# Attention products with v on eight 64x32 tiles, and row maxima packed into five banks

## The chip, the cores and the metric

The kernel runs on one core of a Trainium2 chip. The metric is the device time of one execution, in microseconds. Engines are named as in the profile: PE (TensorE, the matrix products), PEld (its weight loads), DVE (VectorE), ACT (ScalarE), POOL (GpSimd) and SP (SyncE, which here issues most transfers). PSUM, where products land, has eight banks of 512 fp32 columns on 128 partitions.

## The reference

Two layers, each an attention block and a feed-forward block, on 2048 rows of width 640. The attention has 32 heads of width 20 and a causal window of 256 keys.

```python
def _A_ref(x, wqkv, wo):                      # attention
    qkv = (x @ wqkv).reshape(B, S, 3, H, Dh)  # H = 32, Dh = 20
    scores = einsum("bhqd,bhkd->bhqk", q, k) * (Dh ** -0.5)
    mask = (i_q - i_k >= 0) & (i_q - i_k < 256)
    p = softmax(where(mask, scores, -1e9))
    o = einsum("bhqk,bhkd->bhqd", p, v)
    return o.reshape(B, S, D) @ wo

def _B_ref(x, w1, b1, w2, b2):                # feed-forward, F = 1536
    r = relu(x @ w1 + b1)
    return (r * r) @ w2 + b2

x = A_x
for _ in range(2):
    x = x + _A_ref(layernorm(x), A_wqkv, A_wo)
    x = x + _B_ref(layernorm(x), B_w1, B_b1, B_w2, B_b2)
```

## The kernel before

The rows are cut into units of 256; units 0 to 7 are the first layer and 8 to 15 the second. In a unit u with u % 8 != 0 a query sees keys of the unit before and of its own; units 0 and 8 start the sequence and see their own keys only. Heads go in groups of four, called a quad here and in the code; there are eight quads in a unit. A quad's four heads are two values of j (columns of a step) by two values of e (the lower or upper 64 partitions, where its q and k lie, 60 rows deep: each value is kept as fp16 parts).

Each quad goes through three steps:

- `max_quad` (the maxima): scores with queries on the partitions. For each of the four w (j and half i of the unit's queries) and each e, 128 queries by 384 keys land in PSUM, a mask is added and DVE takes the row maximum (L592, `tensor_tensor_reduce` over 384 columns). They use two tiles `bb` of three banks each (`bb6`, handed out by `banks()`, which waits for every earlier reader). From unit 2 on they run on four 64x64 tiles of the array (L570), each with the 320 keys that its 64 queries can see; in unit 1 on the whole array (L579).
- `exp_quad` (the scores for the exponentials): scores again, transposed, keys on the partitions, with the negated maxima as two more rows (L647 on four tiles, L655 on the whole array). ACT takes the exponential out of PSUM (L669), POOL zeroes the masked corners (L684, L688). It uses the same six banks.
- `pv_quad` (the products with v): for each block of 128 keys kb and each of the four heads a product of 32 columns of v (20, one for the sum, the rest unused) with the exponentials, in fp32, on four 128x32 tiles (L718). All of it accumulates in one bank `pv`, which ACT copies to `ot` (L730); every second quad SP writes `ot` out. `steps_of` gives the blocks of keys: first block 1 of the unit before (256 queries), then block 0 of the unit before and block 3 (the second block of the own unit), 128 queries each, then block 2 (the first of the own unit), 256.

Between these steps the dense products of other units run: q, k and v of the unit after, the output product and the feed-forward block of the unit before (`mm3`, L261). The order on every engine is written out by a planner in the program itself: `post` puts a job with an estimated cost on a list, `pump` issues jobs in the order of estimated times and priorities, `need` moves the estimated time on until a job is done. The engines then run their orders as fast as the data allows. In `together` a quad's turn is: `exp_quad(n)`, a share `SHARE` of the dense products, `max_quad` for a quad some way ahead, `pv_quad(n)`, the rest of the dense products. Six banks belong to `bb`, two to everything else (`mm_tile`).

`by_tiles` sorts a quad's products so that the one whose tile has the fewest columns queued so far comes first:

```python
for k, (tile, cols, put) in enumerate(pieces):
    order.append((at.get(tile, 0), k, put))
    at[tile] = at.get(tile, 0) + cols
for _, _, put in sorted(order, key=lambda o: o[:2]):
    for e in range(2):
        put(e)
```

Of the kernel before, what the change touches and what calls it, by code (L numbers as in the profile page):

```python
# [16 lines left out]
P = 128  # L17
S = 2048
D = 640
F = 1536  # L20
H = 32
DH = 20
# [22 lines left out]
def kernel(ctx: ExitStack, tc: tile.TileContext, x, wqkv, wo, w1, b1, w2, b2, out):  # L45
# [18 lines left out]
                            fill=NEG, base=2 * P, channel_multiplier=1)  # L64
    b1s = sb.tile([P, FC], F32, name="b1s")
# [288 lines left out]
    def ln_t(u, yT=None):  # L354
        ys = lns.pop(u)
        if yT is None:
            yT = sb.tile([P, 2, KC, T], F16, name="yT", tag="yT", bufs=1)
        yTs[u], pre[u] = yT, []
        bb = banks() if u == 0 else (None, None)
        for i in range(2):  # L360
            yield from split_t(ys[i][0], yT[:, :, :, i * P:(i + 1) * P], ys[i][1], pre[u], bb[i])
# [156 lines left out]
    bb6 = [ps.tile([P, 3, 512], F32, name=f"bb{e}") for e in range(2)]  # L518

    def banks():  # L520
        need(*bbjobs)
        bbjobs.clear()
        return bb6
# [5 lines left out]
    def by_tiles(pieces):  # L529
# [5 lines left out]
        for _, _, put in sorted(order, key=lambda o: o[:2]):  # L535
            for e in range(2):
                put(e)

    def max_quad(n):

        u, qd = divmod(n, NQ)
        g = u % NG
        qt, cur, prev = qts[u], kts[u % 3], kts[(u - 1) % 3]
# [5 lines left out]
        bb = banks()  # L549

        pieces = []
        for w in (3, 0, 1, 2):
            j, i = divmod(w, 2)
            p = 2 * qd + j
            parts = [(prev, 0, T, 0), (cur, 0, P, T)] if i == 0 else [(prev, P, T, 0), (cur, 0, T, P)]
            if g == 0:
                parts = parts[1:]
            if w == 3:
                parts = [(kt, z, z + P, c + z - a) for kt, a, b, c in parts for z in range(a, b, P)]
            if quarters(u):  # L560
                for kt, a, b, c in parts:
                    for h in range(2):
                        a_, b_ = max(a, a + P // 2 * h - c), min(b, a + 5 * P // 2 + P // 2 * h - c)
                        c_ = c + a_ - a

                        def put(e, kt=kt, a=a_, b=b_, c=c_, h=h, w=w, p=p, i=i):
                            r, rows = slice(64 * e, 64 * e + 3 * DH), slice(64 * h, 64 * (h + 1))
                            to = (bb[e][rows, c // P, 3 * P + c % P:3 * P + c % P + b - a] if w == 3
                                  else bb[e][rows, w, c:c + b - a])
                            nc.tensor.matmul(to, qt[r, p, i * P + 64 * h:i * P + 64 * (h + 1)], kt[r, p, a:b],  # L570
                                             start=True, stop=True, tile_position=(64 * e, 64 * h))

                        pieces.append((h, b_ - a_, put))
                continue
            for kt, a, b, c in parts:
                for e in range(2):
                    r = slice(64 * e, 64 * e + 3 * DH)
                    to = bb[e][:, c // P, 3 * P:] if w == 3 else bb[e][:, w, c:c + b - a]
                    nc.tensor.matmul(to, qt[r, p, i * P:(i + 1) * P], kt[r, p, a:b], start=True, stop=True)  # L579
        by_tiles(pieces)  # L580
        now[0] += (763.0 if quarters(u) else 870.0) if g else 440.0
        for w in range(4):
            j, i = divmod(w, 2)
            o = (0 if g else T if i == 0 else P)
            for e in range(2):
                accum = mx[:, e, (2 * qd + j) % (2 * GQ), i:i + 1]
                if w == 3:
                    v, mask = bb[e][:, o // P:, 3 * P:], maskb[:, o:].rearrange("p (a n) -> p a n", n=P)
                else:
                    v, mask = bb[e][:, w, o:3 * P], maskb[:, o:]  # L590
                bbjobs.append(post("D", 113 + 1.047 * (3 * P - o), lambda v=v, mask=mask, accum=accum:
                                   nc.vector.tensor_tensor_reduce(out=v, in0=v, in1=mask, scale=1.0, scalar=-3.0e38,  # L592
                                                                  op0=ALU.add, op1=ALU.max, accum_out=accum),
                                   prio=urgency["turn"]))
# [32 lines left out]

    def exp_quad(n):
# [3 lines left out]
        bb = banks()  # L632
# [4 lines left out]
        for k, st in enumerate(steps):  # L637
            o = 0
            for kb, kt, ko, q0, qn in st:
                w = qn * P  # L640
                for j in range(2):
                    for h in range(2 if quarters(u) else 0):
                        a, b = (0, w - 64 * (1 - h)) if kb < 2 else (64 * h, w)

                        def put(e, k=k, kt=kt, ko=ko, q0=q0, j=j, h=h, o=o, a=a, b=b):
                            r, rows = slice(64 * e, 64 * e + 3 * DH + 2), slice(64 * h, 64 * (h + 1))
                            nc.tensor.matmul(bb[e][rows, k, o + a:o + b],  # L647
# [4 lines left out]
                        pieces.append((h, b - a, put))  # L652
                    for e in range(0 if quarters(u) else 2):
                        r = slice(64 * e, 64 * e + 3 * DH + 2)
                        nc.tensor.matmul(bb[e][:, k, o:o + w], kt[r, 2 * qd + j, ko:ko + P],  # L655
# [5 lines left out]
        for k, st in enumerate(steps):  # L661
            pts, ms = [], []
            for e in range(2):
# [3 lines left out]
                def power(k=k, e=e, o=o, box=box):  # L667
                    box["pt"] = sb.tile([P, 512], F32, name="pt", tag="pt", bufs=6)
                    nc.scalar.activation(box["pt"][:, :o], bb[e][:, k, :o], AF.Exp, scale=SCALE / (QS * QS))  # L669

                ex = post("A", 50 + 0.834 * o, power, prio=urgency["turn"])
                bbjobs.append(ex)
# [31 lines left out]
    def pv_quad(n, quad):  # L704
        u, qd = divmod(n, NQ)
        steps = steps_of(u)
        pv, jobs = mm_tile([P, T], "pv")
        for k, pts in enumerate(quad[0]):
# [27 lines left out]

        jobs.append(post("A", 262, out, prio=0))
        if qd % 2:
# [395 lines left out]
```

## Time and profile before

| what | value |
|---|---|
| median of 3 runs | 1613.28 us (1612.49 to 1613.58) |
| profiled execution | 1611.7 us, of it a span of 1609.9 us from the first to the last instruction |
| PE busy, share of the span | 1573.4 us, 98% |
| DVE, ACT, POOL busy | 65%, 46%, 38% |
| granted TensorE clock | 1.0 |
| DMA | 158.56 MB, 98 GB/s on average |

A row of the profile gives the line of the program, the engine, the operation, what it writes and reads by the program's names, the shape and the number of records; then the busy time, the mean length of one in ns and the idle time of the engine ahead of it with what ended it. A product's row also gives the tile of the array (rows * columns). An fp32 product is recorded as two. Records of products overlap, so that a mean length is longer than the distance from one to the next. "Issue" in a chain is time in which an engine waited for nothing that the profile shows.

### The profile page before, as it was taken

The numbers are of one execution on the slowest core, as the hardware profiler recorded it, in microseconds if no ns is written. First come the engines' busy times: TensorE is split into PE (matmuls) and PEld (weight loads), VectorE is DVE, ScalarE is ACT, GpSimd is POOL, SyncE is SP. The second block draws the span as 40 slices with busy tenths as digits, with TensorE's granted clock in tenths as the row PEclk, the third lists the DMA queues.
The fourth block names the chain that finished last, engine by engine and source line by source line (L and its number), as shares of the span: only waits on it lengthen the run. The fifth ranks groups of instructions, "written<-read, shape, count | busy, mean of one in ns | idle before, by whom it ended". The sixth has DMA issues, their size and how long they took to land.

```text
span 1609.9 us, 51896 instructions
## 1 busy us (share of the span) xinstructions
PE 1573.4 (98%) x21222; PEld 1178.3 (73%) x21222; DVE 1044.4 (65%) x3250; ACT 734.3 (46%) x1593; POOL 610.9 (38%) x1288
## 2 busy tenths in 40 slices
PE   8998999999999999999999999999999999998999
PEld 7676767777777777777777777777777777775667
DVE  8786865666757657665556766567675666757441
ACT  4554535344453444545343453534545444453522
POOL 1224434235353443535223352533534334353512
PEclk9999999999999999999999999999999999999999
DMA  9763243352434424343352534334343352431020
GB/s 270 206 169 103 60 121 80 99 127 50 120 84 111 97 67 119 74 121 80 95 133 54 122 80 124 81 95 111 66 115 86 107 109 52 111 73 55 27 65 18
DMA packets 234246, 158.56 MB, mean 98 GB/s; under 512 B 82200, under 2 KB 217752, under 8 KB 234008
## 3 DMA queue, kind: packets, MB, share of 16 engines
q1 hardware_dynamic: 227640, 145.74, 37.2%
q10 hardware_dynamic: 6368, 9.50, 2.0%
q8 instruction: 167, 2.74, 0.8%
q14 instruction: 71, 0.58, 0.1%
HBM read 84.68 MB, written 52.95 MB: 85 GB/s over the span
## 4 chain that ended last, share of the span: by engine, by line
PE 90%; DVE 4%; ACT 3%; issue 1%; DMA 1%; POOL 1%; SPq 0%; DVEq 0%; POOLq 0%; ACTq 0%
PE acc L261 67%; PE pv L718 10%; PE bb L647 4%; PE bb L570 4%; DVE bb L592 2%; ACT pt L669 1%; PE spin L275 1%; PE tr L605 1%; PE bb L655 1%; PE bb L579 1%; DMA od<-o 0%; ACT r L889 0%; DVE mx L592 0%; POOL pt L688 0%; DVE mT L610 0%
## 5 line engine op out<-in xcount | busy, mean ns | idle before, releaser
L592 DVE CUSTOM_DVE_ANT_0 bb<-bb,maskb 128x384 f32<-128x384 f32 (+2 forms) x1024 | 510.6, 566 | 101.0 <-PE bb L570 76.1
L669 ACT ACTIVATE pt<-bb 128x512 f32<-128x512 f32 (+1 forms) x736 | 375.8, 601 | 231.2 <-PE bb L647 199.5
L684 POOL TENSOR_SCALAR_AFFINE_SELECT pt<-pt 128x256 f32<-128x256 f32 x448 | 196.9, 445 | 556.2 <-ACT pt L669 534.3
L261 PE MATMUL acc<-y,w_s 128*128 128x256 f16 x2880 | 330.4, 273 | 4.5 <-DVE y L311 1.5
L261 PE MATMUL acc<-w_s,hh 128*128 128x320 f16 x2304 | 326.2, 299 | 0.0
L261 PEld LDWEIGHTS <-w_s 128*128 128x128 f16 x2880 | 277.4, 98 | 57.2 <-issue 23.5
L261 PEld LDWEIGHTS <-hh 128*128 128x128 f16 x2304 | 221.6, 98 | 96.9 <-issue 12.5
L261 PEld LDWEIGHTS <-wq_s 128*128 128x128 f16 x2400 | 230.6, 98 | 45.7 <-issue 15.2
L261 PE MATMUL acc<-yT,wq_s 128*128 128x256 f16 x2250 | 258.9, 273 | 3.6 <-ACT ot L730 1.6
L688 POOL TENSOR_SCALAR_AFFINE_SELECT pt<-pt 128x256 f32<-128x256 f32 x512 | 218.9, 450 | 94.0 <-ACT pt L669 93.1
L899 DVE TENSOR_TENSOR hh<-r,hh 128x256 f16<-128x256 f32 x192 | 92.6, 505 | 201.3 <-ACT hh L896 195.0
L718 PE MATMUL pv<-pt,vt 128*32 128x128 f32 (+1 forms) x3840 | 186.7, 329 | 2.7 <-DVE x L828 1.7
L893 POOL TENSOR_TENSOR r<-r 128x256 f32<-128x256 f32 x192 | 113.5, 612 | 179.0 <-ACT r L889 177.6
L730 ACT COPY ot<-pv 128x256 f32<-128x256 f32 x128 | 47.6, 372 | 276.6 <-PE pv L718 276.5
L592 DVE DVE_READ_ACCUMULATOR2_ANT mx<- 128x1 f32 x1024 | 144.4, 141 | 0.0
L261 PE MATMUL acc<-wo_s,od 128*128 128x320 f16 x960 | 138.7, 300 | 2.1 <-ACT od L801 1.3
L261 PE MATMUL acc<-wq_s,yT 128*128 128x320 f16 x900 | 132.2, 299 | 3.6 <-DVE y L311 1.9
L718 PEld LDWEIGHTS pv<-pt,vt 128*32 128x32 f32 x3840 | 103.5, 109 | 44.0 <-POOL pt L688 5.7
L889 ACT ACTIVATE r<-acc,b1s 128x256 f32<-128x256 f32 x192 | 80.5, 471 | 98.6 <-PE acc L261 95.8
L261 PEld LDWEIGHTS <-od 128*128 128x128 f16 x960 | 91.4, 98 | 44.7 <-issue 6.0
L261 PEld LDWEIGHTS <-yT 128*128 128x128 f16 x900 | 86.6, 98 | 41.1 <-issue 10.5
L298 POOL TENSOR_TENSOR bmv<-bmv,neghalf 128x1 f32<-128x1 f32 x64 | 43.8, 691 | 138.7 <-DVE bmv L292 137.9
(86 smaller groups left out, 1229.0 us busy)
## 6 DMA issues: line engine op xcount, KB each, us to landing
qt<-qk SPq DMA_DIRECT2D x30, 480.0 KB
kt<-qk SPq DMA_DIRECT2D x30, 480.0 KB
qk<-qd SPq DMA_DIRECT2D x17, 640.0 KB
o<-ot SPq DMA_DIRECT2D x256, 42.0 KB
od<-o SPq DMA_DIRECT2D x14, 640.0 KB
qk<-yl SPq DMA_DIRECT2D x13, 640.0 KB
qk<-qd SPq DMA_DIRECT2D x17, 320.0 KB
xt<-in_A_x_dram SPq DMA_DIRECT2D x16, 320.0 KB
```

Source lines behind the costliest of these rows:

```text
L261: nc.tensor.matmul(acc, lhs(a, c), rhs(b, c), start=(k == 0), stop=(k == 3 * nk - 1))
L570: nc.tensor.matmul(to, qt[r, p, i * P + 64 * h:i * P + 64 * (h + 1)], kt[r, p, a:b], start=True, stop=True, tile_position=(64 * e, 64 * h))
L592: nc.vector.tensor_tensor_reduce(out=v, in0=v, in1=mask, scale=1.0, scalar=-3.0e38, op0=ALU.add, op1=ALU.max, accum_out=accum),
L647: nc.tensor.matmul(bb[e][rows, k, o + a:o + b], kt[r, 2 * qd + j, ko + 64 * h:ko + 64 * (h + 1)], qt[r, 2 * qd + j, q0 * P + a:q0 * P + b] ...
L669: nc.scalar.activation(box["pt"][:, :o], bb[e][:, k, :o], AF.Exp, scale=SCALE / (QS * QS))
L684: nc.gpsimd.affine_select(out=m, in_=m, pattern=[[0, 2], [-1, P]], compare_op=ALU.is_gt, fill=0.0, base=0, channel_multiplier=1)
L688: nc.gpsimd.affine_select(out=m, in_=m, pattern=[[0, 2], [1, P]], compare_op=ALU.is_ge, fill=0.0, base=0, channel_multiplier=-1)
L718: nc.tensor.matmul(pv[32 * jj:32 * (jj + 1), q0 * P:(q0 + qn) * P], vf[:, c:c + 32], pj[:, j, :], start=(k == 0), stop=(k == len(steps) - ...
L730: nc.scalar.copy(ot[:, qd % 2], pv)
L889: nc.scalar.activation(box["r"], acc[:, f, :], AF.Relu, bias=b1s[:, f0 + f:f0 + f + 1], scale=1.0 / (YS * WS))
L893: nc.gpsimd.tensor_tensor(box["r"], box["r"], box["r"], op=ALU.mult)
L899: nc.vector.tensor_sub(hh[:, 1, f, :], box["r"], hh[:, 0, f, :])
```

## The change

**Products with v.** In units with u % 8 != 0 the keys of a block are split into two halves h of 64 partitions, and each half has its own bank: the lower half `pv`, the upper half `sixth`. There are eight tiles of 64 rows by 32 columns, one for each half and head. Each half streams only the queries that can see it (`seen`, the windows that the exponentials' scores have already). After ACT's copy of `pv` to `ot`, a new DVE job adds `sixth` to it; the output write waits for that addition.

**Banks.** The two tiles of three banks become one of five (`five`) and one of one (`sixth`). The scores for the exponentials use them as before (`sbank`), but the last bank has a list of readers of its own (`sixjobs`, awaited by `last_bank`).

**Maxima.** In units with u % 8 != 0, unit 1 now included, the eight results of a quad are packed: 320 columns each instead of 384, in five banks, where the second half of the queries sees keys shifted by 64, so that one packed mask (`maskq`, made once) serves all. A result can cross a bank. One bank holds results of both e; the products that write it for one e run first (`TURN`), and 256 columns of w = 0 are left for later: `rest`, called at the head of the next `pv_quad`, runs them on 64x32 tiles ahead of the products with v and posts the eight maxima. So their DVE jobs are posted in `pv_quad`, after all products of the maxima.

**Share.** `SHARE` goes from 0.55 to 0.52, so that less dense work lies between the scores and the maxima, and more behind the products with v.

The diff, cut to its core:

```diff
+    maskq = sb.tile([P, 5 * Q], BF16, name="maskq")
...
-    bb6 = [ps.tile([P, 3, 512], F32, name=f"bb{e}") for e in range(2)]
+    five = ps.tile([P, 5, 512], F32, name="five")
+    sixth = ps.tile([P, 512], F32, name="sixth")
+    flat = five.rearrange("p a n -> p (a n)")
+    sbank = [[five[:, 0], five[:, 1], five[:, 2]], [five[:, 3], five[:, 4], sixth]]
...
+    TURN = ((3, 2, 1, 0), (1, 2, 3, 0))
+    LATER = 4 * Q
+    def max_pieces(n, e, w, x0, x1, m):
...
+        p, at, r = 2 * qd + j, 5 * Q * (4 * e + w), slice(64 * e, 64 * e + 3 * DH)
+        cuts = sorted({x0, x1, *(z - at for z in range(0, 5 * 512, 512) if x0 < z - at < x1)})
...
+                            nc.tensor.matmul(flat[t * m:(t + 1) * m, o:o + b - a],
+                                             qt[r, p, i * P + t * m:i * P + (t + 1) * m],
+                                             kt[r, p, a + to:b + to], start=True, stop=True,
+                                             tile_position=(64 * e, t * m))
...
     def max_quad(n):
...
+        if u % NG:
...
+            by_tiles([x for e in range(2) for w in TURN[e]
+                      for x in max_pieces(n, e, w, LATER if w == 0 else 0, 5 * Q, Q)])
+            now[0] += 656.0
+            def rest():
+                by_tiles([x for e in range(2) for x in max_pieces(n, e, 0, 0, LATER, P // 4)])
+                now[0] += 110.0
+                for e, w in ((0, 3), (1, 3), (0, 2), (1, 2), (0, 1), (1, 1), (0, 0), (1, 0)):
+                    reduce(flat[:, 5 * Q * (4 * e + w):5 * Q * (4 * e + w + 1)], maskq, accum[e, w], 5 * Q)
+                mxjobs[u, G] = list(bbjobs)
+            rest_of.append(rest)
+            return
...
+    def seen(kb, h, w):
+        return (0, w - Q * (1 - h)) if kb < 2 else (h * Q, w)
...
     def exp_quad(n):
-        bb = banks()
+        banks()
+        last_bank()
...
-                bbjobs.append(ex)
+                (sixjobs if (k, e) == (2, 1) else bbjobs).append(ex)
...
     def pv_quad(n, quad):
+        while rest_of:
+            rest_of.pop()()
         pv, jobs = mm_tile([P, T], "pv")
+        if u % NG:
+            last_bank()
+            two = (pv, sixth[:, :T])
+            for k, pts in enumerate(quad[0]):
+                need(*quad[1][k])
...
+                                    nc.tensor.matmul(two[h][32 * jj:32 * (jj + 1), q0 * P + a:q0 * P + b],
+                                                     vf[h * Q:(h + 1) * Q, c:c + 32], pj[:, j, a:b], start=(kb == 1),
+                                                     stop=(k == len(steps) - 1), skip_group_check=True,
+                                                     tile_position=(h * Q, 32 * jj))
+                                pieces.append(((h, jj), b - a, put))
+                by_tiles(pieces)
+                now[0] += 410.0
...
+        def add():
+            nc.vector.tensor_tensor(ot[:, qd % 2], ot[:, qd % 2], sixth[:, :T], op=ALU.add)
         jobs.append(post("A", 262, out, prio=0))
+        last = jobs[-1]
+        if u % NG:
+            last = post("D", 345, add, last, prio=0)
+            sixjobs.append(last)
...
-    SHARE = 0.55
+    SHARE = 0.52
```

More of the change, by code (lines that the diff above doesn't have):

```diff
@@ L595, in max_quad @@
+                nc.tensor.matmul(five[:, 3 * e + j, o:o + n_], qt[r, 2 * qd + j, i * P:(i + 1) * P],
+                                 cur[r, 2 * qd + j, :n_], start=True, stop=True)
+        now[0] += 440.0
+        for w in range(4):
+            j, i = divmod(w, 2)
+            for e in range(2):
+                o, n_ = i * P, (i + 1) * P
+                reduce(five[:, 3 * e + j, o:o + n_], maskb[:, 3 * P - n_:], accum[e, w], n_)
         mxjobs[u, G] = list(bbjobs)
@@ L1077 @@
     dma(lambda: nc.sync.dma_start(b1s, b1.rearrange("(c p) -> p c", p=P)), 8192, *ols[0][2], prio=2)
-    while not all(j.end is not None and j.end <= now[0] + LOOK for j in bbjobs):
+    while not all(j.end is not None and j.end <= now[0] + LOOK for j in bbjobs + sixjobs):
         c = next(rest)
```

113 lines of the change are left out of this document (58 added, 55 removed).

## The prediction

> **What bounds the kernel now.** I read the page's busy table and its chain first.
>
> ```profile
> span 1609.9 us, 51896 instructions
> PE 1573.4 (98%) x21222; PEld 1178.3 (73%) x21222; DVE 1044.4 (65%) x3250; ACT 734.3 (46%) x1593; POOL 610.9 (38%) x1288
> PE 90%; DVE 4%; ACT 3%; issue 1%; DMA 1%; POOL 1%; SPq 0%; DVEq 0%; POOLq 0%; ACTq 0%
> PE acc L261 67%; PE pv L718 10%; PE bb L647 4%; PE bb L570 4%; DVE bb L592 2%; ACT pt L669 1%; PE spin L275 1%; PE tr L605 1%; PE bb L655 1%; PE bb L579 1%; DMA od<-o 0%; ACT r L889 0%; DVE mx L592 0%; POOL pt L688 0%; DVE mT L610 0%
> ```
>
> TensorE (PE) holds 90% of the chain that ended last. The products with v (L718) are 10% of it, the maxima (L570) 4%. A busy PE says little by itself, since its records overlap; so I asked for the windows of single units (one block of 256 rows, 97.2 us) and for the longest waits of PE.
>
> ```profile
> 300.00:397.20 97.20, 97.06 (x1400) 72.93 (x1399) 64.43 (x198) 45.40 (x99) 39.54 (x86) 1.00 0.39 95
> 900.00:997.20 97.20, 97.06 (x1400) 72.91 (x1399) 64.42 (x198) 45.40 (x100) 39.54 (x86) 1.00 0.40 95
> PE bb L570 <- ACT pt L669: 3.4, 8, 1.0
> PE bb L647 <- DVE mx L592: 3.4, 9, 1.1
> ```
>
> Columns after the window: its length, then busy us of PE, weight loads, DVE, ACT, POOL, then the granted clock. A steady unit leaves PE 0.14 us idle; beside its own weight loads no engine passes 65 us of 97, and the clock is full. The longest waits for another engine come to 3.4 us in the whole run. So a nanosecond taken from PE's own stream in a steady unit is a nanosecond of the end, as long as the other engines stay ahead. The chain in order of time shows what one quad (four heads) puts into that stream.
>
> ```profile
> 699.96 3.27 PE acc L261 x30
> 703.23 0.68 PE bb L570 x20
> 703.91 1.44 PE pv L718 x32
> ...
> 709.28 0.68 PE bb L647 x27
> ...
> 710.17 5.03 PE acc L261 x37
> ...
> 810.78 0.79 PE pv L718 x16
> ...
> 170.93 0.82 PE bb L579 x17
> ```
>
> Start, length, what, records. Maxima 0.68 us, products with v 1.44 us right behind, dense products, the scores for the exponentials (L647) 0.68 us, dense products again. The last two lines are from other units: a quad at a sequence's start, whose products with v are half as long, and maxima of unit 1, which still use the whole array.
>
> **The change, part by part.** Terms are per quad; 112 of the 128 quads (units 1-7 and 9-15, eight each) take the new form.
>
> Products with v. Before, four 128x32 tiles each stream 768 columns (256+128+128+256) in fp32, in two recorded passes; a quad at a sequence's start streams 384. So (1.44-0.79)/(768-384) = 1.69 ns per column, and 1.44-768x1.69 = 0.14 us does not depend on columns (fill, drain into the next array shape). After, keys are split in halves of 64 rows, eight 64x32 tiles, and each half skips the queries that it cannot see: 192+64+128+256 = 640 columns for one half, 256+128+64+192 = 640 for the other. If all eight stream at once: 640x1.69+0.14 = 1.22 us. No row of before shows eight tiles, nor fp32 on half the rows. The nearest are these:
>
> ```profile
> 703.16 0.76 PE L570 MATMUL bb<-kt,qt 60*64 60x128 f16 x36
> 703.85 1.51 PE L718 MATMUL pv<-pt,vt 128*32 128x256 f32 x32
> 709.21 0.75 PE L647 MATMUL bb<-qt,kt 62*64 62x192 f16 x32
> 703.16 0.57 PEld L570 LDWEIGHTS <-qt 60*64 60x64 f16 x36 [0.21 <-issue]
> 703.85 0.42 PE L718 MATMUL pv<-pt,vt 128*32 128x256 f32 x4
> L718 PE MATMUL pv<-pt,vt 128*32 128x256 f32 x1920 | 153.5, 386 | 2.7 <-DVE x L828 1.7 <-ACT r L889 0.5 <-POOL pt L688 0.3
> ```
>
> L570 and L647 run four 64x64 tiles, two row halves by two column halves. A column of fp16 is (136-109)/64 = 0.42 ns (5.03/37 for 320 columns, 3.27/30 for 256), and both streams have 1280 columns in each tile: 0.54 us. The bursts took 0.68, so row halves with moving data of their own do run together at full rate, and 0.14 us is fixed. Four fp32 column tiles also start together: four records take 0.42 us where one has a mean of 0.386, so starts are about 0.01 us apart. Eight of them stagger the end by at most 0.04 more; I take 0.03. The other unknown is unequal halves: a load queued for a busy tile may hold up the loads for a free one. L647 has the same windows per half and costs no more than L570, which speaks for zero; but there the whole quad is sorted by length, here only each of three steps. If at both boundaries a tile sits out a load of 0.11 us (the mean of L718's load row is 109 ns, quoted below) it costs 0.22. I take 0.03, near L647. Products with v: 1.28 us, bounds 1.22 to 1.47, against 1.44.
>
> Maxima. The columns per tile stay 1280 but split: 1024 in 64x64 tiles, 1024x0.42+0.14 = 0.57 us, then 256 in 64x32 tiles behind the change of shape, 0.11 us. Together 0.68, as now. There are 33+12 products in place of 36; L570 with 36 and L647 with 32 take the same time, so that count is not what costs. The fixed 0.14 holds a drain: the order dense, 64x64, then 128x32 or 64x32, dense has three changes of shape before and after, so it cancels. [...] What is new is fp16 behind which fp32 follows in one shape. The nearest rows:
>
> ```profile
> 31.79 0.98 PE L261 MATMUL acc<-wq_s,yT 128*128 128x320 f16 x6
> 32.60 0.49 PE L323 MATMUL tr<-ident,xt 128*128 128x128 f32 x3
> L718 PEld LDWEIGHTS pv<-pt,vt 128*32 128x32 f32 x3840 | 103.5, 109 | 44.0 <-POOL pt L688 5.7 <-issue 3.6 <-POOL pt L684 0.2
> ```
>
> Six fp16 products of 0.136 from 31.79 end at 32.61, and the fp32 ones start at 32.60: no gap. So I take 0.69 for the maxima, bounds 0.66 (nothing of the second part exposed) to 0.80 (one more load of 0.11). In unit 1 they took 0.82 or a little less on the whole array and become 0.69 too: 8x0.1 = 0.8 us, 0.7 taken.
>
> Feed. A quad's two bursts rise from 36+32 to 45+128 recorded products, each with a load: 346 instructions in about 2 us, 5.7 ns each. In L570's burst 36 loads start within 0.57-0.11 = 0.46 us, with 36 products between them: 6.4 ns for one instruction, and there the tiles' streams set the pace, so the feed may be faster. The row "x4" has four loads and products start in 0.03 us, so bursts come faster still. At 6.4 ns the 346 would take 2.2 us, 0.25 over the sum below. I take nothing, and 2.2 us in all as the bad end, which the bad ends above already exceed.
>
> VectorE. Each maximum reads 320 columns for 384; each quad gets one new addition.
>
> ```profile
> 703.97 0.57 DVE L592 CUSTOM_DVE_ANT_0 bb<-bb,maskb 128x384 f32<-128x384 f32 x1 [1.10 <-PE bb L570]
> 704.45 0.14 DVE L592 DVE_READ_ACCUMULATOR2_ANT mx<- 128x1 f32 x1
> 704.97 0.14 DVE L592 DVE_READ_ACCUMULATOR2_ANT mx<- 128x1 f32 x1
> ...
> 708.82 0.14 DVE L592 DVE_READ_ACCUMULATOR2_ANT mx<- 128x1 f32 x1
> L592 DVE CUSTOM_DVE_ANT_0 bb<-bb,maskb 128x384 f32<-128x384 f32 x896 | 469.3, 591 | 87.7 <-PE bb L570 76.1 <-PE bb L579 9.1 <-ACT pt L669 1.8
> L592 DVE CUSTOM_DVE_ANT_0 bb<-bb,maskb 128x256 f32<-128x256 f32 x64 | 27.2, 463 | 0.0
> L828 DVE SCALAR_TENSOR_TENSOR x<-acc,x 128x320 f32<-128x320 f32 x60 | 29.2, 487 | 18.8 <-PE acc L261 16.7 <-DMA qt<-qk 0.7
> L669 ACT ACTIVATE pt<-bb 128x512 f32<-128x512 f32 x704 | 366.6, 610 | 230.4 <-PE bb L647 199.5 <-PE bb L655 30.6 <-DVE w_s L199 0.3
> ```
>
> A maximum comes every 0.51 us for 384 columns (703.97 to 704.45 to 704.97). A column costs (591-463)/128 = 1.0 ns, so 64 fewer make it 0.45, and eight save 0.51 us. The new addition of 256 PSUM columns is L828's 0.49 less 64 columns, 0.42 us. It waits for the ACT copy of the other half's sums; behind it on VectorE stand the maxima that are left and the evictions of dense products, and the next scores now wait for it too, since they write its bank. In the quad shown the last maximum ended at 708.96 and the scores began at 709.21, 0.25 us of cover. The maxima start no later than now: 0.81 us after the first product (703.97 against 703.16), when both parts are through. VectorE's chain shrinks by 0.51-0.42 = 0.09 us, and SHARE 0.52 for 0.55 moves 0.03 of a quad's dense work, 0.03x(97.2/8-2.8) = 0.28 us, behind the maxima, so the scores get 0.28-0.15+0.09 = 0.22 us more cover. On the other side the exponentials and their masks have 0.28 us less before the maxima; but the maxima no longer need the sixth bank, so they wait for one L669 fewer (0.61 us). The masks gate the products with v step by step, and only the first step meets them 0.28 us sooner. Where an engine other than PE already sets the pace, the saving can be lost:
>
> ```profile
> 1494.57 0.46 DVE bb L592
> ...
> 1498.23 0.79 PE bb L647 x22
> ```
>
> Here, in the last unit, the chain runs through the maxima up to the scores; such a quad gets VectorE's 0.09, not PE's 0.15. A few quads like it at both ends are worth under 1 us; I take zero, with 3 us lost as the bad end (each of twenty end quads losing its 0.15). The output writes on SP's queue start behind the addition, some 0.5 us later; the transfers queued behind them shift by that, and their readers stand a unit later. Two copies for the packed mask run once, about 0.3 us each by the maxima's row, beside the first unit's loads: nothing.
>
> **Sum.** 0.68+1.44 = 2.12 us become 0.69+1.28 = 1.97: 0.15x112 = 16.8 us, and 0.7 in unit 1: 17.5. The profiled execution took 1611.7 us (span 1609.9 and 1.8 around it), which becomes 1594.2. The median of the runs is 1.6 above it: 1595.8. All good ends give 2.12-(0.66+1.22) = 0.24 a quad, 27.6 us with unit 1, or 1585.7; all bad ends for PE, 0.80+1.47, lose 0.15 a quad, or 1629.
>
> **Rivals.** *The halves take turns in fp32* (slower). If the array streams fp32 for one row half at a time, products with v take 2x640x1.69+0.14 = 2.30 us for 1.44, and the run 0.86x112 = 96 us more, with 0.01x112 for the maxima and 0.7 off: 1710. It decides where less than about 86% of the halves' streams overlap, for 1.08x(2-0.86)+0.20 = 1.43. For it: no row has fp32 on 64 rows. Against: row halves overlap in fp16, and column tiles in fp32.
>
> *Unequal halves hold each other up.* One wait of 0.11 us makes products with v 1.36 and saves 0.07 a quad: 1605. Two lose 0.04, or 1617. For it: within a step the halves differ by 64 columns, and the second and third step begin on them. Against: L647's 0.68 us with the same windows.
>
> *Every product costs a fixed time, in whichever tile.* L570's 36 products in 0.68 us are 19 ns each, and 173 of them would be 3.3 us for 2.12: 132 us more, 1745. Against it: those 0.68 us are accounted for by columns and a fixed part, L647 takes the same time with four products fewer, and four fp32 products start within 0.03 us. [...]
>
> *The saving becomes a wait.* If the copy, the addition behind it and the maxima set the start of the scores in steady units as they do in the last, PE waits for what it saves, and only unit 1 gains: 1612. Against: the cover above, which grows.
>
> **Chances.** The forecast 0.68, turns 0.10, unequal halves 0.15, fixed cost 0.02, wait 0.05. The forecast's own range is 1586 to 1605. The range to hold the time 8 times in 10 goes on to the other cases short of the two far ones, 1586 to 1612. About 0.2% (3 us) is what a measurement can tell from no change. Faster by more: 0.68, most of the unequal halves (0.13) and a little of the wait (0.01), 0.82. Within: 0.04, from the wait and the halves. Slower: the two far ones and 0.02 of the halves and the wait, 0.14.
>
> **What would show it.** In the chain of the changed kernel a quad should read about 0.58 us of 64x64 maxima, then 0.11 and 1.28 of 64x32 work, eight fp32 records starting within 0.06 us, and a steady unit of 97.2-8x0.15 = 96.0 us. The maxima's rows should have 128x320 with a mean near 0.53 us (591 less 64), and VectorE one addition per quad near 0.42. Products with v at 2.3 us would prove the turns; at 1.36 or more with gaps at step boundaries the unequal halves; short bursts with PE waiting for VectorE before L647's successor the wait. A steady unit still at 97.2 us would make the forecast wrong.

## The result and the profile after

| | before | after |
|---|---|---|
| median | 1613.28 us (1612.49 to 1615.06, 5 runs) | 1657.34 us (1655.08 to 1661.5, 5 runs) |
| profiled execution | 1611.7 us, span 1609.9 | 1655.08 us, span 1653.4 |
| first scores of unit 2 | 207.6 us | 226.5 us |
| first scores of unit 15 | 1455.7 us | 1494.1 us |
| a steady unit | 97.2 us | 98.4 to 98.5 us |

The change made the kernel slower: 1.028 times [1.026, 1.0299]. Of the 43.5 us between the spans 18.9 are lost before unit 2, 19.5 from there to unit 15 and 5.1 behind that.

From the page of the changed kernel: span, busy times and the chain by engine.

```profile
span 1653.4 us, 61438 instructions
PE 1574.8 (95%) x25926; PEld 1209.9 (73%) x25926; DVE 1091.6 (66%) x3364; ACT 734.2 (44%) x1593; POOL 620.9 (38%) x1288
PE 69%; DVE 18%; ACT 4%; issue 3%; POOL 3%; DMA 2%; SPq 0%; DVEq 0%; ACTq 0%; POOLq 0%
```

PE's share of the chain fell from 90% to 69%, VectorE's (DVE) rose from 4% to 18%. PE's busy time is 1.4 us more although its bursts became shorter; about 20 us of the span ran at half clock (below). A window of one steady unit (columns as in the prediction), and two of PE's waits in the whole run:

```profile
425.10:523.60 98.50, 96.81 (x1730) 75.08 (x1734) 66.97 (x206) 45.25 (x98) 40.24 (x84) 1.00 0.40 95
PE five L684 <- DVE mx L578: 28.4, 34, 2.1
PE five L693 <- DVE mx L578: 7.1, 10, 1.3
```

PE is idle for 1.7 us of the unit where it was idle for 0.14, and the waits of the scores for the maxima are 35.5 us where the same row (L647) had 3.4. What PE itself does in a quad came out nearly as forecast. PE's timeline:

```profile
738.25 0.88 PE L568 MATMUL five<-kt,qt 60*64 60x64 f16 x45
738.94 0.34 PE L765 MATMUL pv<-pt,vt 64*32 64x192 f32 x4
738.96 0.39 PE L765 MATMUL sixth<-pt,vt 64*32 64x256 f32 x4
...
739.99 0.36 PE L765 MATMUL sixth<-pt,vt 64*32 64x192 f32 x3
740.28 4.75 PE L263 MATMUL acc<-wo_s,od 128*128 128x320 f16 x33
744.96 0.63 PE L684 MATMUL five<-qt,kt 62*64 62x192 f16 x23
```

From the first maximum to the first product with v 0.69 us, from there to the dense products 1.34: 2.03 us where before had 2.12. Lower half (`pv`) and upper half (`sixth`) start 0.02 us apart and stream together. They don't do so without a gap. Between the first step and the second (the same quad, products and then weight loads):

```profile
739.27 0.38 PE L765 MATMUL pv<-pt,vt 64*32 64x64 f32 x9
739.47 0.33 PE L765 MATMUL pv<-pt,vt 64*32 64x128 f32 x4
739.39 0.12 PEld L765 LDWEIGHTS sixth<-pt,vt 64*32 64x32 f32 x4
739.46 0.15 PEld L765 LDWEIGHTS pv<-pt,vt 64*32 64x32 f32 x5
```

The second records of the four lower tiles' 64 columns start at 739.33 to 739.34, and such a record's columns take 0.055 us (64 columns at 0.86 ns: the 256 of `sixth` ahead of them take 0.22, from 738.96 to 739.18). One tile goes on at 739.38 (the ninth record), but the other three get their next product from 739.47 on: four loads for the upper half come first. So they stand idle for 0.08 to 0.11 us; three upper tiles lose about 0.08 us in the same way between the second step and the third. The loss of the whole run is on VectorE. Its timeline in the same quad:

```profile
739.24 0.49 DVE L578 CUSTOM_DVE_ANT_0 five<-five,maskq 128x320 f32<-128x320 f32 x1
739.65 0.14 DVE L578 DVE_READ_ACCUMULATOR2_ANT mx<- 128x1 f32 x1
739.83 0.50 DVE L578 CUSTOM_DVE_ANT_0 five<-five,maskq 128x320 f32<-128x320 f32 x1
740.24 0.14 DVE L578 DVE_READ_ACCUMULATOR2_ANT mx<- 128x1 f32 x1
740.42 0.50 DVE L578 CUSTOM_DVE_ANT_0 five<-five,maskq 128x320 f32<-128x320 f32 x1
```

A maximum is two records: the pass over the columns, and the read of its accumulator. The read starts 0.41 us after the pass here, which is the 320 columns doing what they should. But the next pass starts 0.18 us after the read's start, when the read is over. In the kernel before, a read and the next pass have the same start:

```profile
704.45 0.14 DVE L592 DVE_READ_ACCUMULATOR2_ANT mx<- 128x1 f32 x1
704.45 0.60 DVE L592 CUSTOM_DVE_ANT_0 bb<-bb,maskb 128x384 f32<-128x384 f32 x1
```

So a maximum comes every 0.59 us for 320 columns where it came every 0.515 us for 384. In four of the eight quads of a steady unit the next scores now start 0.05 us behind the last maximum's read: VectorE releases them.

### The profile page after: what moved, and what is told of

The parts are those of the page before. It is cut to its first block, busy times and chain, and to the rows that moved or that the text cites. A ratio compares the mean times of both kernels' runs of the same rounds, so it can differ in the third digit from the quotient of the medians.

```text
span 1653.4 us, 61438 instructions
## 1 busy us (share of the span) xinstructions
PE 1574.8 (95%) x25926; PEld 1209.9 (73%) x25926; DVE 1091.6 (66%) x3364; ACT 734.2 (44%) x1593; POOL 620.9 (38%) x1288
## 4 chain that ended last, share of the span: by engine, by line
PE 69%; DVE 18%; ACT 4%; issue 3%; POOL 3%; DMA 2%; SPq 0%; DVEq 0%; ACTq 0%; POOLq 0%
PE acc L263 51%; DVE five L578 10%; PE pv L765 5%; PE five L684 4%; PE five L568 4%; DVE mx L578 2%; ACT pt L707 2%; PE sixth L765 2%; POOL pt L726 2%; DVE hh L972 1%; DVE ot L803 1%; ACT r L962 1%; PE tr L633 1%; PE five L693 1%; DMA o<-ot 1%
## 5 line engine op out<-in xcount | busy, mean ns | idle before, releaser
L578 DVE CUSTOM_DVE_ANT_0 five<-five,maskq 128x320 f32<-128x320 f32 x896 | 445.6, 497 | 105.9 <-PE five L568 84.1
L707 ACT ACTIVATE pt<-five 128x512 f32<-128x512 f32 (+1 forms) x624 | 319.1, 595 | 267.5 <-PE sixth L684 216.3
L722 POOL TENSOR_SCALAR_AFFINE_SELECT pt<-pt 128x256 f32<-128x256 f32 x448 | 203.0, 462 | 545.6 <-ACT pt L707 528.1
L726 POOL TENSOR_SCALAR_AFFINE_SELECT pt<-pt 128x256 f32<-128x256 f32 x512 | 227.5, 466 | 102.2 <-ACT pt L707 94.5
L765 PE MATMUL pv<-pt,vt 64*32 64x256 f32 (+3 forms) x3584 | 169.2, 301 | 5.1 <-DVE x L900 2.9
L765 PE MATMUL sixth<-pt,vt 64*32 64x192 f32 (+3 forms) x3584 | 159.7, 302 | 1.7 <-issue 1.7
L765 PEld LDWEIGHTS pv<-pt,vt 64*32 64x32 f32 x3584 | 101.3, 106 | 18.8 <-POOL pt L726 8.8
```

Source lines behind the costliest of these rows:

```text
L578: bbjobs.append(post("D", 113 + 1.047 * cols, lambda: nc.vector.tensor_tensor_reduce(out=v, in0=v, in1=mask, scale=1.0, scalar=-3.0e38, op ...
L707: nc.scalar.activation(box["pt"][:, :o], sbank[e][k][:, :o], AF.Exp, scale=SCALE / (QS * QS))
L722: nc.gpsimd.affine_select(out=m, in_=m, pattern=[[0, 2], [-1, P]], compare_op=ALU.is_gt, fill=0.0, base=0, channel_multiplier=1)
L726: nc.gpsimd.affine_select(out=m, in_=m, pattern=[[0, 2], [1, P]], compare_op=ALU.is_ge, fill=0.0, base=0, channel_multiplier=-1)
L765: nc.tensor.matmul(two[h][32 * jj:32 * (jj + 1), q0 * P + a:q0 * P + b], vf[h * Q:(h + 1) * Q, c:c + 32], pj[:, j, a:b], start=(kb == 1), ...
```

## The experiments

Theories. **W**: all eight results of a quad now lie in one tile, `five`; a pass that writes the tile waits until the instruction that wrote it last is through, and that is now always the maximum just before it. In the kernel before the two tiles alternate, so each pass waited for the second-last maximum, which is long over. **A**: the new addition on VectorE. **S**: the share of dense work, 0.52 for 0.55. Later two more: **M**, masks that come late, and **C**, PE's clock.

**One tile instead of two, in the kernel before.** Everything else is as before.

```diff
-    bb6 = [ps.tile([P, 3, 512], F32, name=f"bb{e}") for e in range(2)]
+    six = ps.tile([P, 6, 512], F32, name="bb")
+    bb6 = [six[:, :3], six[:, 3:]]
```

> The kernel before with one change: its two tiles of three banks become the halves of one tile of six banks; nothing else is touched. Theory W: the maxima, 384 columns each, go from one every 0.51 us to one every 0.67, PE waits for VectorE ahead of the scores, and the run takes 1640 to 1680 us. Theories A and S, and a slow read across banks: no change, 1612 to 1616.

1681.83 us, 1.0417 times before [1.0402, 1.0433]. VectorE, and PE's waits:

```profile
736.88 0.57 DVE L593 CUSTOM_DVE_ANT_0 bb<-bb,maskb 128x384 f32<-128x384 f32 x1 [1.11 <-PE bb L571]
737.36 0.14 DVE L593 DVE_READ_ACCUMULATOR2_ANT mx<- 128x1 f32 x1
737.53 0.57 DVE L593 CUSTOM_DVE_ANT_0 bb<-bb,maskb 128x384 f32<-128x384 f32 x1
```

```profile
PE bb L648 <- DVE mx L593: 42.3, 54, 2.0
PE bb L656 <- DVE mx L593: 10.4, 13, 1.5
```

The same six banks under one name cost 68 us. The maximum goes from 0.515 to 0.66 us and the next pass starts behind the read (737.36 and 0.14, then 737.53). Products with v, packing, addition and share play no part here, so W is shown, in the kernel before.

**The changed kernel, maxima written to two scratch tiles in turn.** The pass's output is never read, so it need not go back to `five`. The mask is built in place and small tiles are merged to make room.

```diff
+    junk = [sb.tile([P, 5 * Q], BF16, name=f"junk{i}") for i in range(2)]
...
-            out=v, in0=v, in1=mask, ...
+            out=junk[turn_of[0] % 2][:, :cols], in0=v, in1=mask, ...
```

> The maxima write their masked scores to two scratch tiles in SBUF in turn (bf16, never read), instead of back into the five banks. Theory W (a maximum waits for the accumulator read of the one before, because both write one tile): the wait of 0.17 us goes, a maximum comes every 0.45 us instead of 0.59, PE waits little for VectorE, and the run takes 1598 to 1610 us. Theory A (the new addition, or its place among the maxima, delays the scores): no change, 1650 to 1660. Theory S (SHARE 0.52 and the planner's costs place the scores too early): no change or little, 1640 to 1660.

1619.27 us, 1.0028 times before [1.0012, 1.0045]. VectorE:

```profile
440.40 0.48 DVE L588 CUSTOM_DVE_ANT_0 junk<-five,maskq 128x320 bf16<-128x320 f32 x1
440.81 0.08 DVE L588 DVE_READ_ACCUMULATOR2_ANT mx<- 128x1 f32 x1
440.81 0.48 DVE L588 CUSTOM_DVE_ANT_0 junk<-five,maskq 128x320 bf16<-128x320 f32 x1
```

The passes overlap the reads again, 0.41 us each, and 38 us of the 44 are back. But that is 9 us above the upper end of what W let me expect, and no gain over the kernel before: something else is lost.

**The same with one scratch tile** (`junk[0]` each time).

> As the kernel with two scratch tiles, but every maximum writes the same scratch tile. Theory W: the wait for the accumulator read is back, 0.59 us a maximum, 1650 to 1662 us. If it is instead the target (SBUF in bf16 for PSUM in fp32) that makes the difference, this one is as fast as with two scratch tiles. Theories A and S: 1650 to 1660 for both.

1631.58 us in one run. The interval rises to 0.53 us: with the output outside PSUM and nothing else changed, one tile for two costs 0.12 us per maximum and 12 us. That is W again, now in the changed kernel, but 18 us under the range expected for it. The target counts too: with the wait still there, moving the output from PSUM (fp32) to SBUF (bf16) takes the interval from 0.59 to 0.53 us and the run from 1657 to 1632. So of the 38 us 26 came with the target and 12 with the second tile, in this order. In the other order the parts may differ; the changed kernel with two tiles in PSUM was not run.

**No addition.**

```diff
-            last = post("D", 345, add, last, prio=0)
```

> The changed kernel without the addition of the upper half's sums (the sums of the upper halves of the keys are left out of the result). Theory A: VectorE has 0.42 us a quad less and nothing waits for the addition, 1595 to 1610 us. Theory W: VectorE's chain is 0.33 us shorter of some 5, of which at most 0.33 x 100 quads shows: 1625 to 1645. Theory S: about 1650.

1669.52 us in one run: 12 us slower, and the interval stays at 0.592 us. So A doesn't explain the loss. It doesn't follow that the addition costs nothing, because this run changes more than it. Without the job the planner wrote another order for POOL: in unit 4 the fifth quad's masks end 8.20 us after the quad's first scores, where they ended at 7.17 with the addition. The fifth quads' products with v, which wait for these masks (below), take 13 us more over twelve steady units, while PE's waits for the maxima fall from 35.5 to 22.3 us. So the addition probably has a share in those waits.

**The share.** 0.55 in the changed kernel, then 0.55 and 0.58 with the two scratch tiles (`SHARE = 0.55`, `SHARE = 0.58`). By now I had timed every quad: in the two-scratch kernel seven quads of a steady unit have products with v of 1.33 us, but the fifth has 1.92, in every steady unit. The list of the waits of that kernel doesn't name it, since PE's records overlap and PE isn't idle; the chain of that quad shows one piece of 0.76 us where the other quads have 0.20 us (here the changed kernel's fifth quad, then another of its quads):

```profile
481.40 0.76 PE pv L765 x5
...
739.92 0.20 PE pv L765 x2
```

> The changed kernel with SHARE 0.55 for 0.52, nothing else. In the changed kernel the fifth quad of each steady unit has products with v of 1.92 us where the other seven have 1.33: its third step meets masks that POOL finishes late. Theory S (the share moved the products with v ahead of the masks): those 0.59 us go, about 7 us over twelve steady units. Theory W (every maximum waits for the read of the one before): the scores then have 0.28 us less dense work in front of them behind the maxima, so PE's waits for the maxima grow from 35 us to about 50 to 65 us. Net 1660 to 1690; the fifth quad's products with v at 1.33 us is what tells S.

> The changed kernel with the maxima writing into two scratch tiles in SBUF (as in the first run of that kind, 1619 us), now with SHARE 0.55. The maxima there take 0.41 us each, so eight and the addition are 0.4 us shorter than in the kernel before and the scores do not need the larger share. Theory S: the fifth quad's products with v go from 1.92 to 1.33 us, a steady unit from 96.9 to 96.3 us, and the run to about 1612, less if the first units gain as well (1606 to 1613). If the 0.59 us has another cause than the share, 1619 as before.

> The same with SHARE 0.58. Theory S: nothing more to gain in steady units (96.3 us) as long as the maxima are through before the scores; with 0.28 us less dense work behind them, PE's waits for them in steady units would show from here on if the cover of the 0.55 version is under 0.28 us. 1606 to 1618.

Measured 1675.03 us (one run); 1625.29, 1.0075 times before [1.0061, 1.0089]; 1626.61, 1.0072 [1.0048, 1.0095]. S as a cure is refuted: in the changed kernel PE's waits for the maxima grew from 35.5 to 49.5 us, as W says, and with scratch tiles the fifth quad's products with v went only to 1.73 us, not 1.33, while one scores burst in each steady unit now waited 0.25 us for the maxima; the steady unit is mostly 97.0 to 97.1 us, not 96.3. The products with v did move: with share 0.55 the fifth quad's start 6.40 us after its first scores, as in the kernel before (6.39), and with 0.52 at 5.85. But POOL's order moved as well, and its masks end at 7.52 instead of 7.17. What the 0.59 us is, POOL's rows tell, in the kernel before, then in the two-scratch kernel:

```profile
460.30 1.49 POOL L688 TENSOR_SCALAR_AFFINE_SELECT pt<-pt 128x256 f32<-128x256 f32 x3
461.76 0.86 POOL L848 TENSOR_TENSOR x<-x,xt 128x320 f32<-128x320 f32 x1
461.01 1.51 PE L718 MATMUL pv<-pt,vt 128*32 128x256 f32 x32
```

```profile
462.05 1.18 POOL L972 TENSOR_TENSOR r<-r 128x256 f32<-128x256 f32 x2
463.55 1.49 POOL L732 TENSOR_SCALAR_AFFINE_SELECT pt<-pt 128x256 f32<-128x256 f32 x3
463.73 0.34 PE L771 MATMUL pv<-pt,vt 64*32 64x192 f32 x4
...
464.55 0.95 PE L771 MATMUL pv<-pt,vt 64*32 64x256 f32 x6
465.11 0.51 PE L771 MATMUL sixth<-pt,vt 64*32 64x192 f32 x5
```

The masks of the fifth quad stand behind two POOL squares of the feed-forward block. In the kernel before they end at 461.79 and the third step's products start at 461.90: just in time. In the two-scratch kernel they end at 465.04, measured from the quad's first scores the same 7.17 us, but the products with v begin 0.53 us sooner, and the third step waits until 465.1. The 0.59 us add up: 0.53 from the earlier start, 0.17 from the shorter first two steps (0.72 us for 0.89), less the 0.11 that the kernel before had to spare.

**Scratch tiles in the kernel before**, as a price of the cure alone.

```diff
-    ... tensor_tensor_reduce(out=v, in0=v, in1=mask, ...
+    ... tensor_tensor_reduce(out=junk[e][:, o:], in0=v, in1=mask, ...
```

> The kernel before with its maxima writing into two scratch tiles in SBUF and nothing else. Theory W: there a maximum waits for the read of the second-last only, so the interval of 0.515 us is mostly the maximum's own time; the scratch takes it to about 0.47 to 0.48 us. TensorE bounds the steady units, so they stay at 97.2 us; a little is gained at both ends where the maxima set the start of scores (20 quads by 0.3 us at most): 1607 to 1614.

1610.46 us, 0.998 times before [0.9972, 0.9989]. The interval is 0.478 us and the steady unit stays at 97.2: as expected, a little at the ends.

**Holding the products with v back until the masks are due** (M), in the two-scratch kernel with SHARE 0.52:

```diff
+            while quad and what and what[0] == "v" and not all(j.end is not None and j.end <= now[0] + 700.0
+                                                                for j in quad[1][-1]):
+                c = next(dense, None)
+                if c is None:
+                    break
+                step(c)
+                done += c
             if m is not None:
                 max_quad(m)
```

> The same two-scratch kernel without idle products, but a quad's maxima and products with v are held back behind dense products until the masks of its last step are at most 0.7 us ahead. Theory M (the fifth quad's products with v wait 0.59 us for masks that POOL finishes late, because they start 0.55 us earlier than in the kernel before): the fifth quad's products with v go from 1.92 to 1.33 us and a steady unit from 96.9 to 96.4 us; the run gains 6 to 7 us and reaches 1612 to 1614. If the 0.59 us is not the masks, 96.9 and 1619 stay.

1607.38 us, 0.9966 times before [0.9953, 0.9979]: faster than both kernels. One steady unit, and the fifth quad in PE's timeline:

```profile
405.50:501.90 96.40, 96.08 (x1731) 74.62 (x1730) 61.32 (x206) 45.39 (x98) 40.64 (x84) 1.00 0.39 97
```

```profile
460.55 0.88 PE L573 MATMUL five<-kt,qt 60*64 60x64 f16 x45
461.24 0.34 PE L771 MATMUL pv<-pt,vt 64*32 64x192 f32 x4
...
462.58 0.61 PE L267 MATMUL acc<-y,w_s 128*128 128x256 f16 x4
```

The fifth quad's products with v take 1.34 us and a steady unit 96.3 to 96.4. M is shown. Of the 12.2 us between the two spans (1617.6 and 1605.4) 6.9 lie between the first scores of unit 2 and of unit 14, as expected, and 2.9 behind those, where quads had waited up to 1.3 us for masks. The 2.4 us ahead of unit 2 I can't put down to the edit: all of it is there before unit 1, where PE's order is the same in both kernels.

**The clock** (C). In its profiled execution the changed kernel ran 20 us of its span at half clock before its end, the kernel before none. The windows around one such stretch (PE's busy us, then granted clock), and the least busy window of the kernel before:

```profile
106.90:110.30 3.40, 1.00 (x12) 0.54 (x11) 1.65 (x6) 0.76 (x2) 0.00 (x0) 1.00 0.62 190
110.30:113.70 3.40, 2.79 (x54) 1.82 (x57) 2.50 (x6) 1.37 (x4) 2.92 (x4) 0.51 0.11 19
...
218.40:221.80 3.40, 1.80 (x15) 1.46 (x15) 3.40 (x14) 1.61 (x4) 0.00 (x0) 1.00 0.01 3
```

The clock was granted in pieces of 3.41 us (the changed kernel's stretches at half clock before its end last 3.41 us four times and 6.83 once), and a piece in which PE was busy for 1.00 of 3.40 us was followed by half clock; 1.80 of 3.40 was not. To put a price on it: idle products that fill three of the two-scratch kernel's starved windows; the kernel before without its own 40 idle products; and the fillers together with the hold and with the layer norm's transposes of the first and last unit in two tiles.

```diff
+    def keep_busy(n):
+        for k in range(n):
+            nc.tensor.matmul(sixth[:, :P], ident, ident, start=True, stop=True)
```

> The changed kernel with two scratch tiles and SHARE 0.52 (1619 us, 17.9 us of it at half clock), and 16 idle products (identity by identity, each about 0.1 us) at each of three places where PE stood idle right ahead of a stretch at half clock: ahead of the first scores, ahead of unit 1's first products with v, and behind the transposes of the last unit. Theory C (a 3.4 us window in which PE is busy for less than about half is followed by one at half clock): the windows ahead of those three stretches go from 0.30, 0.37 and 0.38 busy to 0.7 or more, the stretches at about 48, 130 and 1571 us go, half clock falls from 17.9 to about 4 us, and the run to 1610 to 1614. If the half clock has another trigger, the stretches stay and the time is 1619 or more.

> The kernel before without its 40 idle products ahead of unit 0's output projection. Theory C: PE's busy share falls under half in a 3.4 us window there, and a stretch of 3.4 or 6.8 us at half clock follows, which the kernel before does not have: 1615 to 1618. If PE is busy over half there without them, no stretch and 1610 to 1614.

> Both edits together, and the layer norm's transposes of the first and last unit with one half in the five-bank tile and the other half in the ring of dense results, so that the second half no longer waits for the eviction of the first. M and C and the one-tile wait add up: 6.5 us from the masks, 5 to 8 us from the clock, 1 to 2 us from the transposes: 1603 to 1608, below the kernel before (1613) and the kernel before with scratch tiles (1610).

The trigger fits. With the fillers the three stretches are gone (17.9 us of half clock become 6.5, 3.1 of them at the very end; the granted clock of the profiled executions goes from 0.995 to 0.999), and without the 40 products the kernel before gets 13.7 us of half clock in its profiled execution, at a granted clock of 0.996 (3.4 of them at 1484.9 us, far from the edit, behind a window that is half busy):

```profile
109.40:112.80 3.40, 0.48 (x13) 0.19 (x6) 3.23 (x5) 2.93 (x6) 2.25 (x3) 1.00 0.81 178
112.80:116.20 3.40, 0.00 (x0) 0.00 (x0) 2.09 (x5) 0.72 (x3) 1.89 (x6) 0.50 1.07 366
```

The times hardly move: 1618.94 us with the fillers against 1619.27 without, and 1614.39 without the 40 products, 1.0001 times before [0.9991, 1.0011]. This is not the clock's price, because the idle products stand in the way themselves. First the fillers in the last unit, then the 40 products of the kernel before with the output projection behind them, then that projection without the 40:

```profile
1568.25 3.74 PE L672 MATMUL sixth<-ident 128*128 128x128 f32 x32
```

```profile
110.64 9.20 PE L275 MATMUL spin<-ident 128*128 128x128 f32 x80
119.67 4.24 PE L261 MATMUL acc<-wo_s,od 128*128 128x320 f16 x30
```

```profile
116.51 5.84 PE L261 MATMUL acc<-wo_s,od 128*128 128x320 f16 x30 [6.64 <-ACT od L801]
```

An fp32 product is two records here (x32 for 16), so that 16 take 3.6 us, 0.11 us a record, and not the 1.6 that the expectation took, and at all three places real products start right behind them. Without the 40 the output projection starts 3.2 us sooner and, in part at half clock, takes 1.6 us longer. What is won and what is lost were not told apart.

The single executions of one kernel hint at the price. The changed kernel took 1655.08, 1657.09, 1657.34, 1661.42 and 1661.5 us at a mean granted clock of 0.994, 0.993, 0.992, 0.990 and 0.991. If the time at half clock is twice the missing share of the span, 0.001 is 3.3 us of it, and each microsecond of it goes with about half a microsecond more in the time. The two-scratch version (1616.85 us at 0.997 to 1622.48 at 0.994) and the held one (1605.24 at 0.998 to 1611.06 at 0.995) go the same way. An execution that is late for another reason would starve PE too, so this shows no cause, and the price of C stays open. By that slope about 5 of the 38 us that the scratch tiles gave back would be the clock's (an estimate, from median clocks of 0.992 and 0.995).

All edits together gave 1612.39, 0.9995 times [0.9986, 1.0004], 5 us worse than the hold alone: unit 2 begins at 216.2 us against 212.6 and one quad of unit 14 waits 1.8 us. In the last unit the moved transposes no longer wait for each other, but the fillers behind them last until 1567.84 us, and the dense products start there. How much is due to the fillers and how much to the moved transposes was not separated.

## Why the prediction was wrong, point by point

- **Products with v**, 1.28 us: measured 1.33, inside the bounds. Eight tiles do stream fp32 at once: their first records start between 738.944 and 738.968. *The halves take turns* is refuted by that and by the burst of 1.33 us where it asks for 2.30; *every product costs a fixed time* by the eight starts alone, which 19 ns each would spread over 0.13 us. The burst says nothing against it, since it holds 64 recorded products, not the 128 that the prediction counted, and 64 at 19 ns are 1.22 us. *Unequal halves* is not: at each step boundary tiles of one half stood idle for about 0.1 us behind loads for the other half, and 1.33 lies between the forecast and that rival's 1.36.
- **Maxima** on PE, 0.69: measured 0.70. **Addition**, 0.42: measured 0.418; what it adds to the waits for the maxima was not separated.
- **The sum on PE**: 0.15 us a quad became 0.093 (2.125 to 2.032), 10.4 us over 112 quads for 16.8. The mis-sized term is the unequal halves, 0.03 us taken and 0.08 to 0.11 seen; the price of a column held (64 columns in 0.055 us a record, two records a product). Where nothing else is late it arrives: a steady unit of the held version has 96.3 us, and 97.2 - 8x0.093 is 96.5.
- **VectorE: the step that failed.** "64 fewer make it 0.45, and eight save 0.51", "the cover above, which grows". The column price was right (the read starts 0.41 us after the pass). The interval was read as columns alone, and that it depends on which tile the maximum before it wrote was not seen, though in the kernel before the read and the next pass have one start (the prediction quoted the reads alone), and the diff put eight results into one tile. Eight maxima became 8x0.592+0.42 = 5.2 us with the addition, for 8x0.515 = 4.1 before; the cover of 0.25+0.22 us did not hold that. "The maxima start no later than now: 0.81 us after the first product" failed too: in the quad shown it is 0.99 (739.24 against 738.25). This is the wait rival's place, the start of the scores, with another mechanism, and it was priced at no gain where the scratch tiles gave back 38 us (1657.3 to 1619.3), 12 of them by ending the wait alone and 26 with the output's move out of PSUM before that.
- **"The masks gate the products with v step by step, and only the first step meets them 0.28 us sooner"**: wrong twice. The fifth quad's products with v start 0.53 us sooner, since dense products move in whole ones, and it is the third step that waits, 0.59 us a unit. This hid most of the saving of a steady unit even without W: 8x0.093-0.59 leaves 0.15 us (two-scratch kernel: 96.9 against 97.2).
- **The ends**, "I take zero, with 3 us lost": 24 us are lost before unit 2 and behind unit 15's first scores. That the wait on the read counts in full there, because VectorE sets the pace of more quads, is likely but was not shown by itself. With both cures the first scores of unit 2 still stand at 212.6 us against 207.6, of which unit 2 gives 4.0 back, and the end is 2.5 us longer from unit 14's first scores on; some 1.5 us of it go with the transposes' two halves, which wait for one another in one tile (5.0 us from the last unit's first transpose to its steady dense products, for 3.5 before). And PE waits 9.5 us for the maxima behind unit 14's first scores, where the two-scratch kernel waits 4.0: the hold moves some of the wait there. This remainder was not taken apart further.

So 61.5 us lie between forecast and result: 38 from the maxima's interval (one tile and PSUM as target together, and what clock goes with them), 12 from the masks (2 of them not accounted for, above), 6 from the products with v being 0.05 us longer, and some 5 at the ends.

## What to carry to other kernels

When a change merges buffers, look at what the framework's order hangs on: here successive writers of one tile waited for each other to the very end, though their addresses differed, and a chain of eight short reductions paid that each time (0.515 us a maximum became 0.66 in the kernel before). Send an output that nobody reads to scratch tiles in turn (1657 us became 1619). And where a gate is met just in time, moving work past it by half a microsecond can turn the saving into a wait, here of 0.59 us a unit, that the list of waits doesn't name, because overlapping records hide it: time each repeated burst and look at the one that differs.

## What the runs showed of the hardware

In a chain of maxima the next pass waited for the accumulator read where both write one tile: 0.533 us a maximum for 0.411 with one scratch tile for two in the changed kernel, 0.658 for 0.515 with one tile for two in the kernel before, so 0.12 and 0.14 us. With two tiles in turn the read and the next pass start together (440.81 us with scratch tiles, 704.45 in the kernel before). A maximum over 320 columns that writes bf16 to SBUF came every 0.411 us, and over 384 columns every 0.478 us for 0.515 with fp32 written back to PSUM.

The first records of eight fp32 tiles of 64x32 start within 0.03 us (738.944 to 738.968) and run together; 64 recorded products in 1.33 us are 21 ns each. Where the halves' columns differ, a tile stood idle for 0.08 to 0.11 us at a step boundary, behind loads for the other half. At a change of the tiles' shape no product started for 0.12 us in the quad shown, of which the columns of the one before take 0.03: the last 64x64 record starts at 738.705 with 64 columns of 0.42 ns, and the first 64x32 record at 738.824. Within the 64x32 shape the last fp16 record starts at 738.940 and the first fp32 one at 738.944. The 0.09 us that are left would be most of the 0.14 us that the prediction takes as fixed in a burst (an estimate from these starts).

The clock of the changed kernel was granted in pieces of 3.41 us, and the piece ahead of half clock was not idle. PE was busy there for 0.48 us (from 134.24 on), 0.97 (106.93), 1.31 (1533.70), 1.35 (1540.53) and 1.73 (35.25). Pieces with 1.67 us (1608.80) and 1.75 (154.72) were followed by full clock, so in this profile the two cases overlap near one half. One stretch went on for a second piece although PE was busy for 2.83 us of its first (110.34). In the kernel before the least busy piece ahead of the last products has 1.80 us (218.41), and its granted clock is 1.0 over the whole span.
